# Attention feeding a mixture of experts on one core: row scatters and the first gathers issued one per attention block

## The chip, the cores and the metric

One core of one Trainium2 chip runs the whole program in one launch. The metric is device time in microseconds (us), median of several executions. Kernels sent together run on the same chip, in rounds with the kernel before. In this study the chip turned out to matter, so I call the chips of the five calls A (first call), B (second) and C (third to fifth); the run list names the chip. Granted TensorE clock: 1.00 is the full clock, 0.50 half of it. A run more than 1.5% above the fastest of its kernel counts as slow; ratios and verdicts (faster, same or slower at 2%, or unclear) use the other, fast runs.

## The reference

Chunked attention with a few memory keys, then a mixture of eight experts in which a local gate may keep the expert of the token before.

```python
for c in range(nc):                          # chunks of 32, context 16 left and 8 right, 8 memory keys
    scores = scale * np.matmul(q_c, k_full.transpose(0, 1, 3, 2))
    a = np.exp(scores - max) ; a = a / (sum(a) + 1e-9)
    out[:, :, c_start:c_end] = np.matmul(a, v_full)
# x = attention's output as (B, S, H*D) = (4, 768, 512)
for b, s:                                    # E = 8 experts, F = 1024
    e = argmax(logits[b, s]) if s == 0 or local_gate[b, s] < 0.5 else prev_e
    out[b, s] = softmax(logits[b, s])[e] * (np.maximum(x[b, s] @ w1[e], 0) @ w2[e])
```
(abridged)

## The kernel before

Attention runs in 32 blocks of 96 tokens (four batches of eight). After each half batch (four blocks) the tokens' experts and their places in a table sorted by expert are worked out, and GpSimd writes the four blocks' rows to that table in DRAM with four indirect DMAs ("scatters"). When two batches are done, five tiles of 128 sorted rows can be read back with indirect DMAs ("gathers"), while attention goes on with the other two. The first gathered tile is transposed on TensorE at a fixed place, after block 29, so that the experts start without a gap.

```python
def route_rows(r, b, half, x):               # four blocks after the half batch
    ...
    for n in range(HALF):                    # HALF = 4: a burst of four
        ins = nc.gpsimd.indirect_dma_start(
            out=x_dram[:, :], out_offset=bass.IndirectOffsetOnAxis(ap=row[:, n:n + 1], axis=0),
            in_=x[0:QB, j + n].bitcast(I32), in_offset=None).ins
        tc.declare_no_dep(ins, group="scatters", ...)      # scatters don't wait for one another
        scatters[b].append(ins)
...
def gathered(tiles, i, after, xs=None):
    ins = nc.gpsimd.indirect_dma_start(
        out=xs.bitcast(I32), out_offset=None, in_=x_dram[:, :],
        in_offset=bass.IndirectOffsetOnAxis(ap=rows[:, i:i + 1], axis=0)).ins
    for a in after:
        for s in scatters[a]:
            tc.add_manual_dep(ins, s.name, ...)            # a gather waits until its rows have landed
...
n = NQB * FORE + HALF + 2                    # 22
plan_at(after, n, plan_begun)
plan_at(after, n + 1, planned)
plan_at(after, n + 2, early_gathered)        # five gathers in a row, block 24
plan_at(after, NB - 3, first_turned)         # transposes of tile 0, block 29
for n in range(NB - 8, NB):
    plan_at(after, n, some_pieces, 1)        # early pieces of the experts' weights
```

## Time and profile before

| | before |
|---|---|
| timed, median of 3 (range) | 504.61 us (503.54 to 506.27) |
| the execution whose trace came with it | 531.86 us, span 530.1, clock 0.962 |
| TensorE busy in that trace | 503.5 us, 95% of the span |
| GpSimd busy | 99.0 us, 19% |

From the page of that trace: the granted clock in 40 slices of the span (tenths of full speed), and the group of the 32 scatters (count, busy us, mean ns of one, idle time of GpSimd before them and what ended most of it).

```profile
PEclk9998897965999999999999999999999999998999
...
L466 POOL DMA_INDIRECT x_dram<-x,row x32 | 29.6, 926 | 103.3 <-DVE x L464 80.3
```

The clock dips in slices 4 to 10, which is where attention has its bursts; afterwards every slice but one, near the end, reads 9, which means 90% or more. The scatters themselves are short, and GpSimd mostly idles before them. The stages and one burst are shown in the prediction.

### The profile page before, as it was taken

To read this page: it belongs to the slowest core of one execution; us is meant where nothing else is said; L and a number is where in the kernel's file an instruction comes from. 1 tells how busy PE (TensorE), PEld (TensorE's weight loads), DVE (VectorE), ACT (ScalarE), POOL (GpSimd) and SP (SyncE) were. 2 spreads that over 40 slices of the span, in tenths; PEclk is the share of its full clock that TensorE was granted. 3 is DMA by queue.
4 is the path that set the end of the run, shared out by engine and by line. 5 is a ranking of instruction groups with operands and counts; after the bars stand their busy time and mean duration, and the time that the engine had idled before them with its cause. 6 is when DMAs were issued, how large, how long until landed. Compare 5 with 4: busy or idle time off the path is not lost. (4 is left out here: it accounts for less than half of the span.)

```text
span 530.1 us, 9234 instructions
## 1 busy us (share of the span) xinstructions
PE 503.5 (95%) x3474; PEld 387.1 (73%) x3474; DVE 109.6 (21%) x437; ACT 110.6 (21%) x234; POOL 99.0 (19%) x151
## 2 busy tenths in 40 slices
PE   8998989889899999999999999999999999988995
PEld 5998777778766877777677777777766876947772
DVE  2454554644444700000100000000001000000000
ACT  4554353423211111101111011111110111110100
POOL 3002211431305212222200111111100230301000
PEclk9998897965999999999999999999999999998999
DMA  8987776799599998999999999998139935688000
GB/s 298 373 275 207 216 236 189 225 392 382 196 378 302 356 376 310 357 349 344 374 321 337 348 320 322 329 323 335 40 120 413 408 140 172 227 337 324 23 21 23
DMA packets 49377, 146.01 MB, mean 275 GB/s; under 512 B 7258, under 2 KB 11358, under 8 KB 49312
## 3 DMA queue, kind: packets, MB, share of 16 engines
q1 hardware_dynamic: 42240, 123.38, 66.1%
q0 software_dynamic: 6784, 21.30, 11.1%
q8 instruction: 34, 0.56, 0.4%
q10 hardware_dynamic: 288, 0.52, 0.3%
q14 instruction: 31, 0.25, 0.1%
HBM read 132.57 MB, written 13.00 MB: 275 GB/s over the span
## 5 line engine op out<-in xcount | busy, mean ns | idle before, releaser
L644 PEld LDWEIGHTS h_ps<-held_xt,w_sb 128*128 128x128 f32 x704 | 80.5, 192 | 6.6 <-issue 4.9
L644 PE MATMUL h_ps<-held_xt,w_sb 128*128 128x128 f32 x704 | 81.3, 275 | 0.9 <-ACTq _compat.py:109 0.9
L644 PE MATMUL y_ps<-w_sb,ht 128*128 128x512 f32 x176 | 77.5, 593 | 0.0
L796 POOL DMA_INDIRECT out_dram<-y,to x24 | 24.3, 1011 | 257.9 <-ACT y L795 227.7
L791 PE MATMUL y_ps<-w_sb,ht 128*128 128x512 f32 x160 | 70.5, 592 | 0.0
L780 PEld LDWEIGHTS h_ps<-gxt,w_sb 128*128 128x128 f32 x576 | 65.8, 192 | 3.9 <-issue 3.8
L780 PE MATMUL h_ps<-gxt,w_sb 128*128 128x128 f32 x576 | 66.3, 275 | 0.0
L644 PE MATMUL o_ps<-vt,pt 128*96 128x65 f32 x512 | 58.8, 274 | 4.9 <-issue 3.9
L644 PEld LDWEIGHTS o_ps<-vt,pt 128*96 128x96 f32 x512 | 55.1, 189 | 8.1 <-issue 5.8
L644 PEld LDWEIGHTS y_ps<-w_sb,ht 128*128 128x128 f32 x176 | 32.6, 190 | 36.9 <-issue 36.4
L791 PEld LDWEIGHTS y_ps<-w_sb,ht 128*128 128x128 f32 x160 | 29.5, 190 | 33.0 <-issue 32.8
L783 ACT ACTIVATE ht<-h_ps 128x512 f32<-128x512 f32 x42 | 25.1, 597 | 125.3 <-PE h_ps L780 51.9
L466 POOL DMA_INDIRECT x_dram<-x,row x32 | 29.6, 926 | 103.3 <-DVE x L464 80.3
L710 DVE COPY held_xt<-g_ps 128x512 f32<-128x512 f32 x13 | 8.9, 688 | 152.4 <-PE g_ps L644 137.9
L644 PEld LDWEIGHTS s_ps<-qt,kt 64*128 64x128 f32 x512 | 32.1, 197 | 9.5 <-issue 6.3
L644 PE MATMUL s_ps<-qt,kt 64*128 64x96 f32 x512 | 35.4, 287 | 2.2 <-issue 1.8
L644 PEld LDWEIGHTS h_ps<-x,w_sb 128*128 128x128 f32 x192 | 31.2, 190 | 1.2 <-issue 1.2
L644 PE MATMUL h_ps<-x,w_sb 128*128 128x192 f32 x192 | 31.9, 327 | 0.0
L348 ACT ACTIVATE pt<-s_ps,mask_mid 128x256 f32<-128x256 f32 x72 | 28.1, 482 | 17.5 <-remote 9.2
L358 DVE TENSOR_TENSOR x<-o_ps,rinvs 96x256 f32<-96x256 f32 x64 | 26.2, 417 | 1.2
L795 ACT ACTIVATE y<-y_ps,x 128x512 f32<-128x512 f32 x12 | 8.3, 688 | 83.1 <-PE y_ps L644 76.3
L366 ACT COPY xt<-xt_ps 128x384 f32<-128x384 f32 x32 | 15.5, 483 | 47.4 <-PE xt_ps L644 30.1
(207 smaller groups left out, 349.7 us busy)
## 6 DMA issues: line engine op xcount, KB each, us to landing
w_sb<-in_w_dram SPq DMA_DIRECT2D x192, 512.0 KB
vt<-in_v_dram SPq DMA_DIRECT2D x32, 260.0 KB
kt<-in_k_dram SPq DMA_DIRECT2D x30, 256.0 KB
qt<-in_q_dram SPq DMA_DIRECT2D x32, 192.0 KB
kt<-in_k_dram ACTq DMA_DIRECT2D x2, 256.0 KB
x_dram<-x,row POOLq DMA_INDIRECT x32
out_dram<-y,to POOLq DMA_INDIRECT x24
x<-x_dram,rows_late POOLq DMA_INDIRECT x11
```

What stands on the lines that cost most here:

```text
L348: nc.scalar.activation(pt[:, :, :, c], st[:, :, :, c], ACT.Exp, bias=m[:, g:g + 1], scale=SCALE)
L358: nc.vector.tensor_tensor(x[:, 0:D].rearrange("p (a u d) -> p u a d", u=2, d=DH)[:, u], o_ps[:, :, 0:DH], rinv.to_broadcast([QB, HP, DH]), ...
L366: nc.scalar.copy(xt, xt_ps)
L466: ins = nc.gpsimd.indirect_dma_start(out=x_dram[:, :], out_offset=bass.IndirectOffsetOnAxis(ap=row[:, n:n + 1], axis=0), in_=x[0:QB, j + n ...
L644: return lambda *a, **k: tc.keep_in_program_order(f(*a, **k))
L710: nc.vector.tensor_copy(xt[:, :, 0:P], g_ps)
L780: nc.tensor.matmul(h_ps[:, m], lhsT=w1_sb[:, kk, P * (g + m):P * (g + m) + P], rhs=xt[:, kk, 0:rows], start=(kk == 0), stop=(kk == DK - 1))
L783: nc.scalar.activation(ht[:, g:g + many], h_ps, ACT.Relu)
L791: nc.tensor.matmul(y_ps, lhsT=ht[:, m, 0:P], rhs=w2_sb[:, m], start=(m == 0), stop=(m == FK - 1))
L795: nc.scalar.activation(y, y_ps, ACT.Copy, scale=xs[:, D:D + 1])
L796: return nc.gpsimd.indirect_dma_start(out=out, out_offset=bass.IndirectOffsetOnAxis(ap=to, axis=0), in_=y, in_offset=None, bounds_check=NT ...
```

## The change

Its intent: no bursts. Each scatter waits for the values of a different block, and the five gathers are asked for one per block from block 26 on in place of all at block 24. The core of the diff (the tail's bookkeeping cut):

```diff
+            paced[0] = nc.vector.tensor_tensor(      # in values(): the block's last product
...
-        for n in range(HALF):
-            ins = nc.gpsimd.indirect_dma_start( ...
+        r["row"] = row
+        scatter(r, b, j, 0)
+
+    def scatter(r, b, j, n):
+        ins = nc.gpsimd.indirect_dma_start( ... )
+        behind(ins, paced[0].name)                   # held back by that block's values
+        tc.declare_no_dep(ins, group="scatters", ...)
...
         plan_at(after, n + 4, rows, b, half)
+        for j in range(1, HALF):
+            plan_at(after, n + 4 + j, lambda b=b, half=half, j=j: scatter(routes[b], b, HALF * half, j))
...
-    plan_at(after, n + 2, early_gathered)
+    for i in range(EARLY):
+        plan_at(after, n + 4 + i, early_gathered, i)
```

More of the change, by code (lines that the diff above doesn't have):

```diff
@@ L357, in values @@
             nc.vector.reciprocal(rinv, o_ps[:, :, DH:VW])
-            nc.vector.tensor_tensor(
+            paced[0] = nc.vector.tensor_tensor(
                 x[:, 0:D].rearrange("p (a u d) -> p u a d", u=2, d=DH)[:, u], o_ps[:, :, 0:DH],
-                rinv.to_broadcast([QB, HP, DH]), op=ALU.mult)
+                rinv.to_broadcast([QB, HP, DH]), op=ALU.mult).ins
     def turned(x, xt):
@@ L392, in everything, with behind @@
     scatters = {b: [] for b in range(B)}
+    paced = [None]
+    def behind(ins, name):
+        tc.add_manual_dep(ins, name, mybir.DependencyInfo(
+            mybir.DependencyClass.Sync, mybir.DependencyReason.DATA), reason="rows written, or one a block")
     def begin_route():
@@ L464, in route_rows @@
         nc.vector.tensor_tensor(x[0:QB, j:j + HALF, D:D + 1], prob, tot, op=ALU.mult)
-        for n in range(HALF):
-            ins = nc.gpsimd.indirect_dma_start(
-                out=x_dram[:, :], out_offset=bass.IndirectOffsetOnAxis(ap=row[:, n:n + 1], axis=0),
-                in_=x[0:QB, j + n].bitcast(I32), in_offset=None).ins
-            tc.declare_no_dep(ins, group="scatters", query=mybir.DependencyQuery.ANY_SYNC, reason="rows are unique")
-            tc.add_to_no_dep_group("scatters", ins)
-            scatters[b].append(ins)
+        r["row"] = row
+        scatter(r, b, j, 0)
+    def scatter(r, b, j, n):
+        x = xs[b]
+        ins = nc.gpsimd.indirect_dma_start(
+            out=x_dram[:, :], out_offset=bass.IndirectOffsetOnAxis(ap=r["row"][:, n:n + 1], axis=0),
+            in_=x[0:QB, j + n].bitcast(I32), in_offset=None).ins
+        behind(ins, paced[0].name)
+        tc.declare_no_dep(ins, group="scatters", query=mybir.DependencyQuery.ANY_SYNC, reason="rows are unique")
+        tc.add_to_no_dep_group("scatters", ins)
+        scatters[b].append(ins)
     def totals(name, batches):
@@ L607, in gathered @@
             for s in scatters[a]:
-                tc.add_manual_dep(ins, s.name, mybir.DependencyInfo(
-                    mybir.DependencyClass.Sync, mybir.DependencyReason.DATA), reason="rows written")
+                behind(ins, s.name)
         tc.add_to_no_dep_group("scatters", ins)
@@ L698, in planned, with early_gathered @@
         early["pieces"] = [p for ps in pieces for p in ps]
-    def early_gathered():
-        early["xs"] = [gathered(early["tiles"], i, range(FORE)) for i in range(EARLY)]
+    def early_gathered(i):
+        early.setdefault("xs", []).append(gathered(early["tiles"], i, range(FORE)))
     def rows_turned(tiles, i, xs, ps=None, xt=None):
@@ L870, in everything @@
     after.setdefault(NB, []).insert(0, lambda: turn(NB - 1))
-    left = [f for n in range(NB, NB + HALF + 3) for f in first.pop(n, []) + after.pop(n, [])]
-    (TURN, EXPERTS_0, RANKS_0, PLACES_0, LOGITS, ROWS_0, TURNED, PICKS, EXPERTS_1, RANKS_1, PLACES_1,
-     ROWS_1) = left
-    between = {0: {1: [TURN], 3: [LOGITS], 4: [EXPERTS_0], 5: [TURNED], 6: [RANKS_0, PLACES_0, PICKS]},
-               1: {0: [ROWS_0], 1: [EXPERTS_1], 2: [RANKS_1, PLACES_1], 7: [ROWS_1]}}
+    left = [f for n in range(NB, NB + HALF + 6) for f in first.pop(n, []) + after.pop(n, [])]
+    (TURN, MOVE_2, EXPERTS_0, MOVE_3, RANKS_0, PLACES_0, LOGITS, ROWS_0, TURNED, MOVE_4, PICKS, MOVE_5, EXPERTS_1,
+     MOVE_6, RANKS_1, PLACES_1, ROWS_1, *MOVES) = left
+    between = {0: {0: [MOVE_2], 1: [TURN], 2: [MOVE_3], 3: [LOGITS], 4: [EXPERTS_0], 5: [TURNED],
+                   6: [RANKS_0, PLACES_0, PICKS]},
+               1: {0: [ROWS_0], 1: [EXPERTS_1, MOVE_4], 2: [RANKS_1, PLACES_1, MOVE_5], 3: [MOVE_6],
+                   7: [ROWS_1, *MOVES]}}
     late = None
```

## The prediction

> **What bounds the kernel now.** I read the stages first (busy time by window), then each engine's waits inside the attention stage, then the order of time around one burst, and last the untraced times beside the traced span.
>
> The windows below are cut at the instant at which each half batch's row numbers are ready (the scatters of four blocks can start). Columns: window; its length; busy time and count for TensorE, its weight loads, VectorE, ScalarE and GpSimd; granted clock; DMA share; GB/s.
>
> ```profile
> 10.00:43.50 33.50, 33.09 (x424) 30.32 (x422) 17.40 (x66) 20.02 (x50) 0.00 (x0) 1.00 0.93 310
> 43.50:61.50 18.00, 16.61 (x166) 14.27 (x165) 9.07 (x37) 7.48 (x19) 3.76 (x4) 0.81 0.71 206
> 61.50:77.50 16.00, 13.30 (x167) 11.93 (x165) 9.11 (x38) 7.48 (x19) 3.88 (x5) 1.00 0.79 236
> 77.50:95.70 18.20, 16.61 (x167) 14.44 (x166) 9.65 (x42) 7.48 (x19) 3.69 (x4) 0.81 0.71 202
> 95.70:116.40 20.70, 16.96 (x173) 14.72 (x171) 11.32 (x59) 7.38 (x19) 8.51 (x9) 0.88 0.90 307
> 116.40:136.40 20.00, 19.71 (x151) 18.12 (x149) 9.70 (x40) 5.40 (x13) 3.73 (x4) 0.62 0.83 317
> ...
> 144.00:371.00 227.00, 226.54 (x1341) 167.62 (x1338) 30.70 (x111) 30.48 (x50) 45.24 (x56) 1.00 0.95 341
> ```
>
> Three stages. Up to 43.5 us there is no scatter, and 424 matmuls take 33.5 us: 79 ns each, at full clock. From 43.5 to 136.4 us there is one burst of scatters in every window (five gathers more in the fifth); 166+167+167+173+151 = 824 matmuls take 18.0+16.0+18.2+20.7+20.0 = 92.9 us, 113 ns each, with the clock down to 0.62. At 79 ns the 824 would take 65.1 us, so in this trace the stretch holds 27.8 us of excess. From 144 to 371 us the DMA share is 0.95 at 341 GB/s: the experts' weights stream, 192 pieces of 512 KB, and the matmul count per us is low. The weight stream for the third tile starts at 137.0 us, when attention ends and its buffers come free. So attention is bound by TensorE, the experts by the weight stream, and what shortens attention moves all that follows nearly one for one.
>
> Now the order of time at the first burst: start, duration, engine, line, operation; in brackets idle time and what ended it.
>
> ```profile
> 45.18 0.92 POOL L466 DMA_INDIRECT x_dram<-x,row  x1 [0.30 <-issue]
> ...
> 46.40 0.92 POOL L466 DMA_INDIRECT x_dram<-x,row  x1 [0.31 <-issue]
> ...
> 47.63 0.92 POOL L466 DMA_INDIRECT x_dram<-x,row  x1 [0.30 <-issue]
> 48.13 0.33 PEld L644 LDWEIGHTS o_ps<-vt,pt 128*96 128x96 f32 x3 [0.39 <-issue]
> 48.15 0.37 PE L644 MATMUL o_ps<-vt,pt 128*96 128x65 f32 x2 [0.26 <-issue]
> 48.86 0.22 PE L644 MATMUL o_ps<-vt,pt 128*96 128x65 f32 x1 [0.34 <-issue]
> 49.57 1.29 PEld L644 LDWEIGHTS o_ps<-vt,pt 128*96 128x96 f32 x9 [1.11 <-issue]
> 49.58 1.47 PE L644 MATMUL o_ps<-vt,pt 128*96 128x65 f32 x9 [0.50 <-issue]
> 49.65 0.33 SPq L263 DMA_DIRECT2D qt<-in_q_dram  x1
> 49.72 1.21 ACT L348 ACTIVATE pt<-s_ps,mask_mid 128x256 f32<-128x256 f32 x3 [3.63 <-remote]
> ```
>
> TensorE drips one or two matmuls every 0.72 us while it waits for nothing that the trace shows, ScalarE sits 3.63 us, and TensorE, SyncE and ScalarE come free within 0.15 us of each other, 1.0 us after the last scatter's descriptors are done (48.55). The same end shows at the other bursts: descriptors done at 82.57, TensorE free at 83.67; done at 110.06, free at 111.23. After two of the first three stalls the clock drops to 0.50 (49.9 to about 54, 84 to 89), and after the gathers it stays there until about 131. Nothing is held by data: all three engines are stopped together.
>
> **Is the stall there without tracing?** The traced execution took 531.86 us, the timed ones have a median of 504.61: 27.2 us that tracing adds. The excess just worked out is 27.8 us. The trace has a second sign: before 40 us every VectorE semaphore update that the instructions call for is on record (15 of 15, 15 of 15, 12 of 12, 30 of 30 per 10 us); from 40 to 50 us it is 16 of 25, from 60 to 70 us 15 of 28, from 100 to 110 us 14 of 33. So records are lost just where the engines stop[...].
>
> [...] 0.50 follows stalls of about 2 to 3 us with a drip in them. [...] descriptors take 0.92 us, while the copy of the row tokens that needs a burst's landing waited 3.36 us after its last issue.
>
> **The change part by part.** It adds no work: 32 scatters of 0.92 us and five early gathers of 0.96 us stay. Removed: the run of four scatters at 1.23 us spacing, 4.9 us a burst, and the five gathers from 104.0 to 110.1. Added: for each scatter a wait for the values of a block; VectorE's product there is done in any case, so GpSimd, 19% busy, waits and no one waits for GpSimd. Moved: a half batch's last scatter goes three blocks later. At 79 ns and about 165 matmuls per four blocks, a block is 3.3 us; so one 0.92 us scatter in 3.3 us, about 28% of GpSimd. Where the next half batch's scatters meet the gathers (blocks 26 to 30), two in 3.3 us, still under 2 us.
>
> The gathers move from block 24 to blocks 26 to 30. The first has to land before the transposes set after block 29. Its last scatter is issued after block 25 and lands some 3.4 us later, about block 26's end; the gather's own landing, some 3 to 5 us more with the weights on the queues, is near block 28. That leaves about one block, 3 us: on no path if the estimate holds. After attention the last half batches' scatters follow no new block, so they come as before, in bursts inside the first two expert tiles; their readers, the late gathers, stood at 180.6 us and are needed three tiles later.
>
> What is gained depends on the stall alone. In the trace: five windows' excess, 27.8 us, less the planning work in the fifth (about 1.5 us) and what remains where gather and scatter meet (3 to 6 us), so 18 to 23 us off the traced span, to about 508 to 512. In the timed runs: if 27.2 of the 27.8 us of excess are tracing's own, 0.6 us is left to gain; if half is real, about 10 us; if all, 20.
>
> **The rivals.** First, the stall is real in untraced runs[...]. For it: a DMA's own semaphore updates in the trace drip at the same 0.7 us (48.34, 48.90, 49.61), and the change's author saw enough in the bursts to pace them. Against it: records are lost there, and then the 27.2 us of tracing would have to come from the weight stream, of which I see no sign. It would give 485 to 495 us. Second, the bursts slow the attention's loads (packets of the load queue took up to 0.95 us in the burst against 0.085): they are issued four blocks ahead, 13 us, and only 1.8 and 1.2 us of TensorE's weight-load waits name a load; worth under 1 us. Third, a new wait: the first gather lands late, behind 8 MB of early weights at a DMA share of 1.0 from 105 to 130 us, and the pinned transposes hold TensorE, 2 to 6 us, perhaps with a cold clock after it: 507 to 514 us. Fourth, an instruction fetch starved by the scatters: the fetches (16 KB each, at 40.9, 55.1 and 69.5 us) fall in no stall, so it is out.
>
> **Range and chances.** I give the tracing account about two thirds, with 503.5 us; a stall that is real in part or whole 0.26, with 485 to 496 at its strong end and 498 at its weak one; a late gather 0.07. Faster by 2% means under 494.5 us. The middle is 502 us; 8 in 10 lie between 489 and 507.
>
> **What would show it right or wrong.** Right: in the changed trace the windows' pace in attention falls from 113 to under 90 ns a matmul, GpSimd's scatters stand some 3 us apart, the clock stays near 1.0, attention ends near 117 us instead of 137, and the traced span drops by about 20 us, while the timed median moves by under 1%; the gap of 27 us between traced and timed shrinks. Wrong: the timed median falls by 10 us or more along with the trace (the stall was real), or the traced stalls stay with single scatters (it is not the burst), or TensorE waits before the first tile's transposes.

The marked cuts took out what no trace here shows: statements on the profiler's records, on when the clock falls and on where a DMA instruction ends, and the guesses of a choked record path and of a path that scatters clog. No term of the sum was in them. It stays 503.5 us for the tracing account at about two thirds, 485 to 498 us for a real stall at 0.26 and 507 to 514 us for a late gather at 0.07, with the middle at 502. But the two thirds now stand on 27.2 against 27.8 us and on the missing records (16 of 25, 15 of 28, 14 of 33) alone; the rest of that weight was my estimate. Three readings need a word. A scatter's "descriptors" are its instruction on GpSimd, 0.92 us. The "3.4 us" of a scatter's landing is the wait of 3.36 us in that trace, and the "3 to 5 us" of the gather's own is my estimate from it; I had read no gather's landing. And the 0.95 and 0.085 us of the load queue's packets are the longest and the median between 44 and 49.5 us; from 20 to 40 us, with no scatter yet, that trace has 1.05 and 0.084, so it shows no loads slowed by the burst (counted in the trace file).

## The result, and the profile after

The kernel after takes 517.04 us (516.51 to 518.14, 4 runs) against 504.71 us (503.54 to 506.27, 4 runs): ratio 1.0245, interval 1.0212 to 1.0278, so slower. Ratios here are the mean time of one kernel's fast runs over that of the other's fast runs of the same rounds, so not quite the ratio of the medians that I quote.

The trace of before that I had was no fair partner, as the first experiment shows. So the lines below set the trace of after (518.14 us, span 516.2, chip not on record) beside that of the kernel before on chip A (run before_again: 504.71 us, span 502.8). Busy time by window, columns as in the prediction. The kernel after:

```profile
43.50:61.50 18.00, 17.61 (x226) 16.09 (x226) 12.09 (x57) 9.38 (x25) 6.05 (x6) 1.00 0.88 263
95.70:116.40 20.70, 13.45 (x141) 11.31 (x140) 9.15 (x37) 6.41 (x17) 6.39 (x7) 0.81 1.03 409
116.40:136.40 20.00, 19.84 (x138) 17.49 (x138) 9.84 (x46) 3.93 (x9) 6.96 (x11) 0.77 0.78 282
```

The kernel before on chip A:

```profile
43.50:61.50 18.00, 17.61 (x225) 16.09 (x225) 12.18 (x58) 9.31 (x25) 6.73 (x8) 1.00 0.85 269
95.70:116.40 20.70, 20.02 (x223) 18.12 (x225) 14.16 (x67) 8.33 (x22) 11.04 (x13) 1.00 1.03 385
116.40:136.40 20.00, 20.00 (x138) 15.42 (x131) 9.75 (x36) 3.94 (x8) 5.10 (x9) 1.00 1.03 392
144.00:371.00 227.00, 226.13 (x1335) 167.40 (x1334) 19.94 (x68) 29.52 (x47) 39.93 (x51) 1.00 0.87 321
```

Where the bursts are (first row) the two kernels are equal, 226 and 225 matmuls in 18 us at full clock: on chip A there was nothing in a burst to gain. In the second row the kernel after loses 82 matmuls and the clock falls to 0.81. The last row also corrects a reading of mine: among the experts TensorE is busy for 226.13 of 227 us and the DMA share is 0.87, so that stage is bound by TensorE and not by the weight stream. The prediction's own row for that stage, with 226.54 us of 227 busy, said so already.

What TensorE does at the place of the loss, in order of time (start, duration, operation; in brackets the idle time before it and what ended it). The kernel after:

```profile
105.33 0.50 PE L654 MATMUL xt_ps<-ident,x 96*128 96x96 f32 x4
112.79 1.08 PE L654 MATMUL g_ps<-ident,xs 128*128 128x128 f32 x4 [6.96 <-DMA xs<-x_dram,rows_early]
113.80 1.51 PE L654 MATMUL lt_ps<-xt,wg 128*32 128x384 f32 x8
...
123.31 3.00 PE L654 MATMUL h_ps<-held_xt,w_sb 128*128 128x128 f32 x16
126.14 0.49 PE L654 MATMUL xt_ps<-ident,x 96*128 96x96 f32 x4
```

The kernel before on chip A:

```profile
105.42 0.50 PE L644 MATMUL xt_ps<-ident,x 96*128 96x96 f32 x4
106.02 0.65 PE L644 MATMUL g_ps<-ident,xs 128*128 128x128 f32 x4
106.60 0.85 PE L644 MATMUL lt_ps<-xt,wg 128*32 128x384 f32 x8
...
112.00 1.98 PE L644 MATMUL h_ps<-held_xt,w_sb 128*128 128x128 f32 x16
113.82 0.49 PE L644 MATMUL xt_ps<-ident,x 96*128 96x96 f32 x4
```

TensorE comes to the transposes of the first gathered tile at 105.8 us and waits 6.96 us for the gather; before, the tile was there. And after the wait the same work takes nearly twice as long (1.51 us for the eight logits matmuls in place of 0.85), because the clock is at half from 108.4 us, some 2.5 us into the wait, until 125.4 us. The sum closes: the transposes start 112.79 - 106.02 = 6.77 us later; from them to the end of the experts' first 16 matmuls (h_ps) 13.35 us pass (112.79 to 126.14) in place of 7.80 (106.02 to 113.82), 5.55 us more. Together 12.3 us. The first tile's output scatter is issued 12.34 us later (142.95 against 130.61), and what follows takes nearly as long as before (373.3 and 372.2 us to the end of the span). The medians differ by 12.33 us, these two executions by 13.4 us.

Why the gather is late, from GpSimd's own order of time in the kernel after:

```profile
93.58 1.38 POOL L476 DMA_INDIRECT x_dram<-x,row  x1 [1.59 <-DVE x L358]
98.44 0.92 POOL L476 DMA_INDIRECT x_dram<-x,row  x1 [3.49 <-DVE x L470]
100.68 0.92 POOL L476 DMA_INDIRECT x_dram<-x,row  x1 [1.32 <-DVE first L412]
106.22 0.99 POOL L614 DMA_INDIRECT xs<-x_dram,rows_early  x1 [4.62 <-issue]
107.69 0.95 POOL L614 DMA_INDIRECT xs<-x_dram,rows_early  x1 [0.48 <-DMA x_dram<-x,row]
```

The last scatter whose rows the gather needs is issued at 93.58 (at 88.1 in before_again) and lands, that is, the last update of its semaphore is on record, 7.3 us later, at 100.9. But the first gather is issued at 106.22 only. The scatter of 98.44 belongs to the next batch, whose rows the gather does not read; it landed at 105.44 (7.0 us), and the one of 100.68 at 107.4, just before the first and the second gather start (0.8 and 0.3 us). The code says why: scatters are exempt from waiting for one another, but a gather reads the same DRAM table, so it waits for every scatter that stands before it in the program, also for those of the next batch: the first gather for one of them, the second for both. Before, the gathers stood ahead of them. Then the gather lands 6.4 us after its issue, at about 112.6. That the gather waits for those scatters is read from the times and the code here; gathers_first and before_gathers_26 test it.

### The profile page after: what moved, and what is told of

Same layout as the page of the kernel before. It is cut to its first block, busy times and chain, and to the rows that moved or that the text cites. A ratio compares the mean times of both kernels' runs of the same rounds, so it can differ in the third digit from the quotient of the medians.

```text
span 516.2 us, 9234 instructions
## 1 busy us (share of the span) xinstructions
PE 493.4 (96%) x3474; PEld 378.8 (73%) x3474; DVE 109.5 (21%) x437; ACT 110.9 (21%) x234; POOL 101.0 (20%) x151
## 5 line engine op out<-in xcount | busy, mean ns | idle before, releaser
L654 PEld LDWEIGHTS h_ps<-held_xt,w_sb 128*128 128x128 f32 x704 | 81.6, 194 | 6.6 <-issue 4.9
L654 PE MATMUL y_ps<-w_sb,ht 128*128 128x512 f32 x176 | 77.5, 593 | 0.0
L654 PE MATMUL o_ps<-vt,pt 128*96 128x65 f32 x512 | 51.7, 256 | 0.1
L654 PEld LDWEIGHTS o_ps<-vt,pt 128*96 128x96 f32 x512 | 48.7, 172 | 2.9 <-DVE base L446 1.2
L476 POOL DMA_INDIRECT x_dram<-x,row x32 | 31.4, 983 | 82.0 <-DVE x L470 48.9
L654 PEld LDWEIGHTS s_ps<-qt,kt 64*128 64x128 f32 x512 | 29.9, 188 | 6.3 <-issue 2.9
L654 PE MATMUL s_ps<-qt,kt 64*128 64x96 f32 x512 | 32.7, 277 | 0.4 <-ACT pt L348 0.4
L808 ACT ACTIVATE y<-y_ps,xs 128x512 f32<-128x512 f32 x12 | 8.2, 687 | 83.1 <-PE y_ps L804 61.8
```

The lines of the kernel that those rows point to most:

```text
L476: ins = nc.gpsimd.indirect_dma_start(out=x_dram[:, :], out_offset=bass.IndirectOffsetOnAxis(ap=r["row"][:, n:n + 1], axis=0), in_=x[0:QB, ...
L654: return lambda *a, **k: tc.keep_in_program_order(f(*a, **k))
L808: nc.scalar.activation(y, y_ps, ACT.Copy, scale=xs[:, D:D + 1])
```

## The experiments

The theory after the result: (1) pacing the scatters gains nothing, (2) the whole loss is the late first gather: TensorE waits, and then works at half clock, (3) it is late because its last scatter is issued later, because it stands behind scatters of the next batch, and because each landing takes 7 us with the weights in the queues. The rivals: pacing has a gain of its own that the late gather hides; the pacing itself costs.

### First call (chip A; before 504.63 us, 503.71 to 505.62, 7 runs)

**before_again**: the kernel before, unchanged.

> The kernel before, unchanged, to read a second traced execution and the spans and clocks of its runs. If tracing is what stops the engines in the bursts, every traced execution is some 27 us longer than the timed ones (about 530 against 504.6 us). If the 531.86 us was one odd execution, this trace will be near 505 us with attention at about 79 ns a matmul in the bursts too.

504.66 us (503.75 to 505.93), ratio 1.0004 (0.9981 to 1.0027). The profiled execution took 504.71 us and shows no stops, with full clock through all of attention. So a trace can be taken without costing 27 us, and my reading that tracing caused the stops is false as it stood. What made the first trace different was open here; chip C answers part of it below.

**turn_later**: the transposes of the first tile two blocks later.

```diff
-    plan_at(after, NB - 3, first_turned)
+    plan_at(after, NB - 1, first_turned)
```

> The changed kernel with the transposes of the first expert tile two blocks later (after block 31, not 29). Theory A (the 12 us are TensorE's 6.96 us wait for the first gather plus the half clock after it, and pacing gains nothing in timed runs): back to the time before, 503 to 507 us, no wait of over 1 us at these transposes, no clock of 0.50 near 110 us. Rival B (pacing slows something else too, such as the late scatters or the weight stream): stays over 510 us. Rival C (the stall of the bursts was real in timed runs): under 495 us.

512.59 us (510.99 to 513.88), ratio 1.0163 (1.0133 to 1.0193). TensorE still waits, 2.95 us for the gather, and half clock follows for 3.4 us: the two blocks give back only part, since this execution's gather was issued at 107.48 and landed at about 115 us. It is 4.5 us under the median of the kernel after and supports the theory's direction, not my size: by the numbers that I had set, over 510 us spoke for rival B, that pacing slows something else too. The trace leaves that rival little. The first output scatter comes at 136.77, 6.2 us later than in before_again, and 5.9 us of it are here: 0.5 from an earlier lag, the 2.95, 0.79 for the copy of the transposed tile that now stands on the path, and 1.70 in the 16 experts' matmuls at half clock (3.68 us in place of 1.98).

**gathers_first**: the kernel after, but the five gathers together at the front of block 26, ahead of the next batch's scatters.

```diff
-    for i in range(EARLY):
-        plan_at(after, n + 4 + i, early_gathered, i)
+        after[n + 4].insert(i, lambda i=i: early_gathered(i))    # ahead of that block's rows
```

> The changed kernel with the five early gathers issued together ahead of block 26's scatter, scatters still one a block. Tests whether the first gather was late because it waits for the landing of the scatter issued just before it, whose rows it does not read. If so, the first gather issues near 101 us in place of 106.2, TensorE's wait falls from 6.96 to 1 to 2.5 us, the clock stays at 1.0 and the time is 504 to 508 us. If the lateness is the queue full of weights alone, the wait stays at 5 us or more and the time over 512 us.

Fast runs 506.98 to 509.18 us (one run of 515.47), ratio 1.007 (1.004 to 1.010). The first gather is issued at 101.47 us, 0.2 us after the landing of its own last scatter (93.75 and 7.5 us), in place of 106.22; TensorE waits 2.57 us and has 3.4 us of half clock. So the place behind the next batch's scatters is worth about 8 of the 12 us, and what is left, the later issue and the long landings of the gather and its own scatters, the other 4. Time and clock lie just outside what I expected.

**burst8**: meant to issue eight scatters in a row.

```diff
+        r.setdefault("ready", []).extend((row, n, j + n) for n in range(HALF))
+        if half == 0:
+            return
-        for n in range(HALF):
+        for row, n, at in r["ready"]:
```

> The kernel before with the scatters of both halves of a batch issued together, eight in a row in place of four. Theory A (the bursts cost nothing in timed runs): timed within 1% of before, 502 to 508 us, whatever its trace shows. Rival C (bursts stop the engines in timed runs too, by 2 to 5 us each)[...], 510 us or more.

505.51 us (503.69 to 506.25), ratio 1.0007 (0.9985 to 1.003). The edit failed: the trace has four and four at the same places as before (43.91 to 47.65, 57.32 to 60.98). Nothing else stood between them in GpSimd's queue, and each scatter waits only for its own rows, so a later place in the program moved nothing. The run counts as another one of the kernel before.

### Second call (chip B; before 504.76 us, 503.69 to 506.31, 7 runs)

**pace_rest**: scatters paced, but the last four before the gathers at once, and the gathers at block 24 as before.

```diff
-        scatter(r, b, j, 0)
+        for n in range(HALF if (b, half) == (1, 1) else 1):
+            scatter(r, b, j, n)
...
-        plan_at(after, n + 4 + i, early_gathered, i)
+        plan_at(after, n + 2, early_gathered, i)
```

> The kernel after, with every scatter paced one to a block except the last four before the gathers (second half of batch 1), which go out at once, and with the five gathers asked for in a row at block 24 as in the kernel before. Theory (late gather alone costs the time; pacing the scatters gains nothing): gather 0 is issued near 94 us, TensorE does not wait for it, first output scatter near 130.5 us, 504.7 us, ratio 0.997 to 1.003. Rival (pacing has a gain of its own that the late gathers hid): 485 to 500 us, first output scatter before 127 us.

504.78 us (503.93 to 505.11), ratio 0.9993 (0.9966 to 1.0021). First gather at 94.45, no wait, first output scatter at 130.83. Pacing all scatters but those four neither gains nor costs on this chip.

**gathers_paced**: bursts kept, only the gathers one per block from block 24.

```diff
-    plan_at(after, n + 2, early_gathered)
+    for i in range(EARLY):
+        plan_at(after, n + 2 + i, early_gathered, i)
```

> The kernel before, bursts of scatters kept, only the gathers paced one to a block from block 24 on. Theory: gather 0 is still issued near 94 us, so the transposes find it; the later gathers come in time too, unless one of them waits behind the scatters of block 26: 504.7 us, ratio 0.997 to 1.008. Rival (pacing of the gathers is itself what costs): 510 to 517 us.

504.92 us (503.66 to 505.86), ratio 1.0008 (0.9978 to 1.0038). The first gather is issued at 93.28; the third to fifth wait behind the next batch's scatters until 109.58, and still nobody waits for them.

**before_gathers_26**: the kernel before, nothing paced, the five gathers at block 26.

```diff
-    plan_at(after, n + 2, early_gathered)
+    plan_at(after, n + 4, early_gathered)
```

> The kernel before, bursts kept and nothing paced, only the five gathers moved from block 24 to block 26, where they stand behind the four scatters of that block. Theory (what costs is the place of the gather, behind scatters that have to land, and not the pacing): gather 0 is issued after 105 us, TensorE waits 6 to 11 us for it at the pinned transposes, goes to half clock after it, 513 to 522 us. Rival (pacing costs): 504 to 507 us.

520.43 us (517.22 to 523.49), ratio 1.0313 (1.0251 to 1.0375). GpSimd's and TensorE's order of time:

```profile
101.33 0.92 POOL L466 DMA_INDIRECT x_dram<-x,row  x1 [0.30 <-issue]
110.51 0.99 POOL L603 DMA_INDIRECT xs<-x_dram,rows_early  x1 [8.26 <-issue]
```

```profile
117.10 1.09 PE L644 MATMUL g_ps<-ident,xs 128*128 128x128 f32 x4 [12.06 <-DMA xs<-x_dram,rows_early]
```

This is the strongest single result: no pacing anywhere, only two blocks' later place, and the kernel before becomes 15.7 us slower (the kernel after lost 12.3). The gathers now wait until the whole burst of the next batch has landed (8.0 to 8.8 us a scatter). With pace_rest this shows that the loss comes from the gather's place, not from pacing.

**stream_held**: the kernel after with the early weight pieces held back to block 29.

```diff
-    for n in range(NB - 8, NB):
-        plan_at(after, n, some_pieces, 1)
+    for n in range(NB - 3, NB):
+        plan_at(after, n, some_pieces, 4)       # and each piece held behind that block's values
```

> The kernel after, with the early expert weights held back to block 29, so that the scatters and the first gathers run without them in the queues. Theory (weights stretch each landing): a scatter lands 3 to 4 us after its issue in place of 6 to 7, gather 0 is issued near 102.5 us and lands near 106, TensorE waits under 1.5 us for it. The total is open: the first tile's weights then come later, 505 to 520 us. Rival (landing time has nothing to do with the weights): gather 0 issued near 106 us and the wait near 7 us as in the kernel after.

511.76 us (510.06 to 513.87), ratio 1.0145 (1.0102 to 1.0188). Issue to landing of the two scatters of blocks 26 and 27, lowest, median and highest; first the kernel after, then stream_held:

```profile
DMA to landing us min/median/max: 6.7/6.9/7.0
```

```profile
DMA to landing us min/median/max: 4.0/4.4/4.8
...
115.03 0.80 PE L656 MATMUL h_ps<-held_xt,w_sb 128*128 128x128 f32 x2 [2.22 <-DMA w_sb<-in_w_dram]
```

Without the weights in the queues a scatter lands in 4.0 to 4.8 us and the first gather (issued at 102.87) in 3.4 us; TensorE idles 0.92 us ahead of the transposes. So these landings are longer with the weights in the queues (6.7 to 7.0 us for the scatters, 6.4 for the gather). The total is better than the kernel after by 5 us only, because TensorE now waits for the weights (the last line; 2.9 us in three waits) and has half clock after it.

### Third call (chip C)

**kept_warm**: the kernel after with 44 unused transposes where TensorE waits. **after_again**: the kernel after.

```diff
+        for kk in range(44 if ps else 0):
+            nc.tensor.transpose(g_ps[:, kk % DK], ident, identity=ident)
```

> The kernel after, with 44 transposes of the identity (about 7 us of TensorE work that nobody uses) put where TensorE waits 6.96 us for the first gather. They end about when the gather lands, near 112.8 us. Theory (the loss of 12.3 us is 7 us of waiting and 5 to 6 us of work at half clock that the waiting caused): the clock stays at 1.00, the waiting is only filled, and 510 to 512.5 us are measured, 5 to 6 us less than the kernel after. Rival (the late gather and the weights behind it cost all 12 us, the clock would have been hidden): 515 to 518 us.

> The kernel after, unchanged, in the same call, for a second trace of it: 516.5 to 518 us, gather 0 issued near 106 us, TensorE waits near 7 us. Open: whether the half clock lasts 12.6 us past the wait again, or 3.4 us, as after the waits of other runs; if it lasts 3.4 us, the time should be near 512 us.

On this chip the kernel before took 529.05 to 543.14 us in all of seven runs, and the kernel after 521.10 us (519.88 and 522.31): ratio 0.9788 (0.9666 to 0.9909). The whole interval lies below 1, but the record's verdict at 2%, from two runs, is "unclear". It still overturned my view that the change never gains, and I spent the rest of the runs on it. For the question asked: after_again waits 8.70 us and then has half clock until about 131 us, so the long half clock repeats. Why it is long is open: in the kernel after TensorE works from 112.79 to 125.4 us, 12.6 us, at half clock with no idle above 0.15 us, while in gathers_first the half clock, from 108.7 us, ends at 112.1, 3.5 us after TensorE is back (108.56). kept_warm takes 514.74 us (508.74 to 518.17, the last of them slow), some 6 us less than the kernel after on the same chip, as expected in difference (its ratio to the kernel before is 0.9613, verdict unclear). But the fill lasted only 5.02 us, TensorE waited 2.31 us more, and the traced run fell to half clock all the same, so the test as planned failed. The best evidence that the clock costs its 6 us is within this kernel: the run with a mean clock of 0.998 took 508.74 us, the two with 0.984 took 514.64 and 514.84.

### Fourth call (chip C again; before 532.08 us, 525.84 to 536.31, 4 runs)

**before_third**, the kernel before, and the kernels of pace_rest, gathers_paced and burst8 again.

> The kernel before, unchanged. On a chip like that of the last call: 529 to 543 us, with more than 100 ns for each matmul between 43.5 and 136.4 us and all engines idle together in the bursts of scatters, as in the first trace. On an ordinary chip: 503.5 to 506.5 us and no stops.

> Scatters one to a block (but the last four before the gathers), gathers in a row at block 24. Theory (on such a chip bursts of scatters stop the engines, and pacing removes the stops; the late gather was the whole loss elsewhere): 504 to 512 us on a chip like that of the last call, 5 per cent under the kernel before there and also under the 521 us of the kernel after; 504.7 on an ordinary one. Rival (the stops on such a chip are not of the bursts): 525 us or more there.

> Bursts of scatters kept, the gathers alone paced. On a chip like that of the last call: theory (bursts of scatters cause most of the stops): 524 to 540 us, at most 5 us under the kernel before. Rival (the burst of five gathers causes them): under 515 us. On an ordinary chip 504.9.

> Scatters of two halves in bursts of eight. On a chip like that of the last call: if the stops grow with the number of scatters in bursts, about the time of the kernel before (as many scatters in bursts), 529 to 545 us; if they grow with the length of a burst, more than that. On an ordinary chip 505.5.

before_third: 535.39 us (531.27 and 539.50; its trace fell in the slower run). pace_rest_2: 514.07 us (510.71 to 518.70), ratio 0.9636 (0.9446 to 0.9825). gathers_paced_2: 527.39 us (523.65 to 534.67), ratio 0.9836 (0.9707 to 0.9964). burst8_2, which is the kernel before once more: 536.40 us (529.28 to 545.62), ratio 1.0055 (0.9844 to 1.0266). The record's verdict on all three is "unclear"; the ratios of the first two lie below 1 with their whole intervals. The medians include slow runs (one of four in each of the first two and in the kernel before, two in burst8_2), the ratios do not. pace_rest_2 lies above the 504 to 512 us that I expected, far below the rival's 525. Windows of two fast runs: gathers_paced_2, which keeps the bursts of scatters,

```profile
43.50:61.50 18.00, 16.57 (x167) 14.35 (x167) 9.10 (x38) 7.48 (x19) 3.75 (x4) 0.81 0.69 209
61.50:77.50 16.00, 14.32 (x142) 12.32 (x142) 8.24 (x35) 5.62 (x15) 3.87 (x5) 0.79 0.68 200
77.50:95.70 18.20, 15.72 (x193) 13.86 (x189) 10.42 (x45) 9.37 (x25) 3.69 (x4) 1.00 0.81 229
```

and pace_rest_2, which has a single burst left, at 84.67 to 88.34 us:

```profile
43.50:61.50 18.00, 17.61 (x228) 16.08 (x227) 11.83 (x56) 9.79 (x26) 6.03 (x6) 1.00 0.87 263
61.50:77.50 16.00, 15.68 (x198) 14.36 (x198) 10.19 (x41) 9.00 (x23) 5.26 (x6) 1.00 0.89 261
77.50:95.70 18.20, 15.59 (x163) 13.82 (x161) 12.30 (x63) 7.74 (x20) 7.34 (x8) 0.85 0.87 268
```

On chip C TensorE loses time where scatters come in bursts of four, and not where they come one per block: 167 and 142 matmuls against 228 and 198 in the first two windows. A second count agrees: between 43 and 101 us the waits of TensorE's matmuls for which the trace names no releaser ("issue") come to 4.1 us in gathers_paced_2, 2.5 in before_third and 1.4 in pace_rest_2, and to none in pace_two and after_again, where scatters come singly or in pairs. Much of the loss is the half clock that follows (mean clock 0.81 and 0.79 in the first two windows of gathers_paced_2, against 1.00). The one burst that pace_rest_2 keeps shows it in its own order of time (third scatter of that burst, then TensorE, VectorE and ScalarE; the last two are put down to TensorE's results):

```profile
87.12 0.92 POOL L477 DMA_INDIRECT x_dram<-x,row  x1 [0.31 <-issue]
...
88.00 0.19 PE L656 MATMUL d_ps<-tiles_early,before 8*8 8x1 f32 x2 [1.20 <-issue]
...
88.92 0.18 DVE L557 COPY sums_early<-s_ps_early 128x17 f32<-128x17 f32 x1 [2.08 <-PE d_ps L656]
...
90.61 2.30 ACT L348 ACTIVATE pt<-s_ps,mask_mid 128x256 f32<-128x256 f32 x6 [2.54 <-PE s_ps L656]
```

Half clock follows from 90.3 to 100.6 us. In the same kernel on chip B the same burst left TensorE busy: 29 matmuls between 86 and 88 us, in place of 9 here, and the clock stayed at 1.00.

### Fifth call (chip C; before as in the fourth call, with four more runs: 532.08 us, 525.84 to 536.31, 8 runs)

**pace_two**: all scatters paced, the last half batch before the gathers as one, one, two over blocks 22 to 24, the gathers in a row behind them. **pace_two_spread**: the same with the gathers one per block from block 24. **gathers_first_2**: the kernel of gathers_first.

```diff
-            plan_at(after, n + 4 + j, ...)
+            plan_at(after, n + 4 + (min(j, 2) if g == 3 else j), ...)
-        plan_at(after, n + 4 + i, early_gathered, i)
+        plan_at(after, n + 2, early_gathered, i)          # pace_two_spread: n + 2 + i
```

> All scatters one to a block, except the last two before the gathers, which go together at block 24; the five gathers in a row behind them. On an ordinary chip: gather 0 issued near 97.5 us, landed by 104, TensorE waits under 1 us, 504 to 507 us. On the chip with stops: theory (the burst of four scatters held the rest) 504 to 510 us and no half clock between 84 and 101 us; rival (the burst of gathers holds it) 511 to 518 us.

> The same with the gathers one to a block from block 24 on. On an ordinary chip: as the former, 504 to 508 us, unless a later gather comes late behind a scatter of block 26. On the chip with stops: if the gathers' burst also stops engines, 3 to 6 us under the former; otherwise the same within 2 us.

> All scatters one to a block, the five gathers in a row at the front of block 26. On an ordinary chip 507 to 509.5 us, as before. On the chip with stops: 508 to 513 us, with the 2 to 3 us wait for gather 0 and no stop in the scatters; above 515 us if the burst of gathers stops the engines.

pace_two: 515.24 us (514.37 to 516.00), ratio 0.9682 (0.9610 to 0.9754). pace_two_spread: 513.90 us (512.00 to 516.07), 0.9640 (0.9565 to 0.9715). gathers_first_2: 517.80 us (514.17 to 519.55), 0.9714 (0.9629 to 0.9800). The theory was right in its place and wrong in the total: pace_two and gathers_first_2 lie where I had put the rival, that the burst of gathers stops engines too, while pace_two_spread gains too little on pace_two (1.3 us, not 3 to 6) for the gathers alone. The stop at 84 to 101 us is gone in pace_two (216 matmuls at clock 1.00 between 77.5 and 95.7 us, against 163 at 0.85). But now the last scatters land late, the first gather is issued at 101.50 in place of 92.79 in pace_rest_2, and around the seven indirect DMAs issued in a row from 101.50 to 109.08 TensorE idles 1.82 and 3.46 us and 1.55 us more before the tile's transposes, and half clock follows. Spreading the gathers shortens that run to four DMAs, two gathers and two scatters, but does not remove it: TensorE idles 2.09 us there. What stops TensorE is open: it idles around seven and around four indirect DMAs in a row here, but the five gathers in a row of pace_rest_2 (92.79 to 97.87 us) left it busy, at half clock, and no run tests their number by itself. How much of the remaining 9 to 11 us over the other chips is stop and how much is lateness I did not separate.

So no version beat the kernel before on chips A and B (in before_again, on A, TensorE is busy for 472.0 of the 485.2 us that were read by window, 97%). Of the kernels tried on both kinds of chip, pace_rest is the best of those that lose on neither: 504.78 us on B and 514.07 us on C, against 504.76 and 532.08 for the kernel before.

## Why the prediction was wrong

The prediction was 502 us with a range to 507; the time is 517.04, 10 us above the range.

**What held.** The paced scatters stand apart as I said (44.13, 46.35, 50.10, 52.68 us), no work was added, and the pace in the first window is under 90 ns a matmul (18.0 us for 226 matmuls, 80 ns). But the kernel before has that pace on chip A too (225), so the change did not bring it, and over the whole stretch from 43.5 to 136.4 us the kernel after needs 101 ns (920 matmuls in 92.9 us). The excess of 27.8 us was well estimated: in before_again the first output scatter is issued 27.2 us earlier than in the trace of before (130.61 against 157.79). The last sign under "Wrong" named what came: TensorE waits before the first tile's transposes. The timed median does not gain from the pacing, as I gave most weight.

**The step that failed.** It is the gather's estimate: "That leaves about one block, 3 us: on no path if the estimate holds." Three of its terms were off. "Its last scatter ... lands some 3.4 us later" was taken from a burst ahead of the weights, and was read wrongly there: 3.36 us passed from the end of that scatter's instruction, 4.3 us from its issue (65.63 to 69.92). There the paced scatters of the kernel after land in 3.6 to 6.2 us (those of 44 to 80 us), but behind the weights this one took 7.3 us. "[T]he gather's own landing, some 3 to 5 us more", an estimate with no gather's landing behind it, took 6.4 us. And the order was not looked at: I counted the gather free as soon as its own rows had landed (100.9 us), while it also waited for a scatter of the next batch, landed at 105.44, and was issued at 106.22. By my terms it would have landed at 93.58 + 3.4 + 5, about 102 us, 4 us ahead of the transposes; it landed at about 112.6. The 10.7 us between are 3.9 of the scatter's landing, 5.3 of the order and 1.4 of the gather's landing.

**The rival that came true.** The third one, "the first gather lands late, behind 8 MB of early weights at a DMA share of 1.0 ... and the pinned transposes hold TensorE, 2 to 6 us, perhaps with a cold clock after it: 507 to 514 us", with a chance of 0.07. The mechanism was right; its size was short by one microsecond in the wait (6.96) and by 5.55 us for the clock, which I had as a perhaps; and its chance followed from the margin just shown to be false.

**The tracing account.** "27.2 us that tracing adds" compared a trace with timed runs that, as far as I can now tell, were not of the same chip. Every run of the five calls comes with a span and a clock, the timed ones too, so all were recorded in some way: on A and B without stops, on C the kernel before was 21 to 38 us slower in every execution (525.84 to 543.14 against 504.7), and its traces taken there have the stops. The traces carry a mark: those of A and B and that of the kernel after hold 7447 to 7461 records of semaphore updates, those of C 6564 to 6746, and the trace I predicted from 6611 (counted in the trace files). So records do go missing with the stops, as I saw; but pace_rest_2 also misses them (6564) while its paced stretch has no stops, and no run shows that the one causes the other. That the first trace came from C or a chip like it is inferred from these counts, its time and its form. Whether the stops would be there without any recording, what makes C different, and whether it is the chip or its state in those three calls, no run here can show. Two readings of that first trace were off besides: the half clock after the first and the third stall lasts to 56.7 and 90.8 us, not to about 54 and 89, so more of the excess is half clock and less is standing still.

**Rival one, the real stall.** False on A and B, whose times of before are those of the runs that the prediction was about: pace_rest is 504.78 us on B. On C the timed runs have it: pacing takes 18 us off by the medians (532.08 to 514.07; 20 by those of the fast runs, 530.85 to 510.73), near the "18 to 23 us off the traced span" that I worked out. But since those runs are recorded too, this does not show the stall in unrecorded ones. On C even the kernel after, with its late gather, is below the kernel before (0.9788, verdict unclear).

**The experts' bound.** "[T]he experts by the weight stream" was read from the DMA share of the disturbed trace (0.95) past TensorE's 226.54 of 227 us in the same row. TensorE is the bound, in the undisturbed trace as well (226.13 of 227 us). The consequence I drew, that what delays attention delays all, holds either way.

## What to carry to other kernels

In this program a gather waited also for earlier writes to its table whose rows it does not read (in the kernel after it was issued 0.8 us after such a write had landed, 5.3 us after its own rows had; in before_gathers_26 it stood behind a burst that took 8.0 to 8.8 us a scatter to land), so before moving one later, list which writes it will then stand behind and take landing times from the stretch where it will run, not from a quiet one (7.3 us with the weights in the queues, 3.6 to 6.2 us ahead of them). A wait of TensorE can cost more than its length: in three runs here half clock came with it, and the loss was 12.3 us for a wait of 6.96 in the kernel after, 15.7 for 12.06 in before_gathers_26 and about 4 for 2.57 in gathers_first. And when a trace's time and the timed median disagree as here (531.86 and 504.61 us; the trace taken again came with 504.71), take the trace again, if possible on another chip, before explaining its form.
